# A branch moved ahead of three sums: where TensorE waits for a flag in a fused attention and gated-MLP kernel

## The chip, the cores and the metric

The kernel runs on one core of a Trainium2 chip, as one launch. The metric is the device time of an execution in microseconds; the median of the runs counts. The engines are named as in the profile: PE is TensorE (PEld its weight loads), DVE VectorE, ACT ScalarE, POOL GpSimd, SP SyncE, which here only issues DMAs. Each has a sequencer of its own that reads instructions and queues them for the engine; the profile writes it with a q (PEldq, DVEq).

## The reference, cut to what matters

```python
def reference(A_x, A_wqkv, A_wo, B_x, B_w1, B_w3, B_w2, gate_w):
    x = A_x                                             # 1 x 2048 x 512
    g = _sigmoid((x * gate_w).sum(-1, keepdims=True))
    a = _A_ref(x, A_wqkv, A_wo)   # attention: 32 heads of 16, softmax(q k^T / 4) v, then wo
    b = _B_ref(x, B_w1, B_w3, B_w2) # (silu(x w1) * (x w3)) w2, with F = 1792
    return g * a + (1 - g) * b
```

Both parts are computed from `A_x`. All data is float32.

## The kernel before, in words

The sequence of 2048 rows is cut into 16 tiles of 128 rows (`NT`) and into 4 blocks of 512 columns (`NB`); D = 512 is 4 chunks of 128 (`ND`). Float32 products are made of three matmuls in a faster format: each operand is split into a high and a low half, and `three` (L96, L97, L98) multiplies high by high, high by low and low by high into one PSUM bank.

The first 80 us are a prologue. It loads and transposes x, projects the first 128 columns of Q and K (`project_qk`, L199), and projects V. One V tile is `sums_v(t)`: 4 chunks by `three`, 12 matmuls with 12 weight loads into one of three PSUM banks named `f`. `project_v(t)` lets ACT copy the bank into V (L227). Tiles 0 to 12 go that way; for the last three, 13 to 15, the sums stand in TensorE's order and DVE copies them (L415).

The softmax needs a bound on the scores. `bound` and `guard_rows` work out a bound from norms and write a `flag` (L250): 1 if the bound is at most 64, so that the scores need no exact row maxima. `values_load` (L411) has every engine's sequencer read the flag into a register. `row_maxima` (L293) is a `tc.If(small < 1)` block: where the flag is 0 it projects the rest of Q and K and computes all scores once for their maxima, a body of thousands of TensorE instructions. With these inputs the flag is 1 and every engine branches past the body. On that path each engine passes instructions of one kind, `EVENT_SEMAPHORE`, which wait for the engine's own count and raise the semaphores by what the skipped body would have added (on SP eight of them, for its DMA semaphores).

What follows is the main part, some 1300 us. An order written out by hand as a string of Q, F and P sets TensorE's stream: Q is a pair of score matmuls (L791, with an exponential on ACT at L795), P the products with V (L779), F the matmuls of the remaining projections and of the MLP (L432, L550). The first is Q. The scores read `Kt` and `Qt`, which SP loads with DMAs (L270, L277, and L282 for the guard rows). The kernel is under `tc.manual_schedule()`: each engine gets its instructions in the order of the text.

The lines around the change, before it:

```python
    load_guard(0, 0, 0)                                              # SP, L282
    project_v(12)
    small = nc.values_load(flag, min_val=0, max_val=1)               # L411
    last_v = [sums_v(t) for t in range(NT - 3, NT)]                  # TensorE: 36 matmuls
    row_maxima(small)                                                # the branch, L293
    for to, src in last_v:
        nc.vector.tensor_copy(to, src)                               # DVE, L415
```

Of the kernel before, what the change touches and what calls it, by code (L numbers as in the profile page):

```python
# [24 lines left out]
NT = S // P  # L25
# [8 lines left out]
def gated_mix_kernel(ctx: ExitStack, tc: tile.TileContext, x, wqkv, wo, w1, w3, w2, gate_w, out):  # L34
# [18 lines left out]
    nc = tc.nc  # L53
# [35 lines left out]
    def bank():  # L89
        return psum.tile([P, 512], F32, name="f", bufs=3)  # L90
# [3 lines left out]
    def three(ps, sH, sL, mH, mL, first, last):  # L94

        nc.tensor.matmul(ps, sH, mH, start=first, stop=False)  # L96
        nc.tensor.matmul(ps, sH, mL, start=False, stop=False)  # L97
        nc.tensor.matmul(ps, sL, mH, start=False, stop=last)  # L98
# [120 lines left out]
    def sums_v(t):  # L219
        ps = bank()  # L220
        b, o = divmod(P * t, 512)
        for k in range(ND):
            three(ps, xH[b][:, k, o:o + P], xL[b][:, k, o:o + P], wv[k][0], wv[k][1], k == 0, k == ND - 1)
        return V[:, t, :, 0:DH], ps.rearrange("p (h d) -> p h d", d=DH)
# [184 lines left out]
    load_guard(0, 0, 0)  # L409
    project_v(12)  # L410
    small = nc.values_load(flag, min_val=0, max_val=1)  # L411
    last_v = [sums_v(t) for t in range(NT - 3, NT)]
    row_maxima(small)
    for to, src in last_v:
        nc.vector.tensor_copy(to, src)  # L415
    ph1.close()
    wk = ctx.enter_context(tc.tile_pool(name="wk", bufs=1))

# [503 lines left out]
```

## Time and profile before

| | us |
|---|---|
| median of 3 runs | 1403.82 (1403.74 to 1717.74) |
| the profiled execution | 1402.91 |
| its span, first to last instruction | 1401.1 |
| TensorE busy | 1394.2 |
| ScalarE busy | 1032.8 |
| VectorE busy | 486.6 |
| GpSimd busy | 321.1 |

The profile shows one execution. The highest of the three runs stands apart from the other two, which agree within 0.1 us. Busy time on TensorE counts a matmul from its start to a modelled end, and successive matmuls overlap; whether TensorE waits is read from the starts of its matmuls. Register, branch and semaphore instructions of the sequencers aren't counted as busy; they appear when a line of the source is asked for by itself.

### The profile page before, as it was taken

How to read it: one execution, taken by the hardware profiler on the slowest of the kernel's cores; microseconds unless marked ns; L12 is line 12 of the kernel's file. 1: busy time of each engine (PE TensorE's matmuls, PEld its weight loads, DVE VectorE, ACT ScalarE, POOL GpSimd, SP SyncE). 2: the span in 40 equal slices, each digit the busy share in tenths (PEclk: the TensorE clock that was granted, in tenths of full speed). 3: DMA queues.
4: the chain of work that ended last, by engine and by line, in shares of the span. 5: the costliest groups of instructions: out<-in, count | busy, mean ns of one | idle time of the engine just before them, and what ended most of it. 6: DMA issues, size and time to landing. Idle time of an engine off the chain costs nothing.

```text
span 1401.1 us, 28802 instructions
## 1 busy us (share of the span) xinstructions
PE 1394.2 (100%) x11398; PEld 819.8 (59%) x11398; DVE 486.6 (35%) x1069; ACT 1032.8 (74%) x1153; POOL 321.1 (23%) x357
## 2 busy tenths in 40 slices
PE   9999999999999999999999999999999999999998
PEld 8866566565565565565565565555555555555556
DVE  5511111564545556555464654411111111110013
ACT  4457677777777777777777777788778878877880
POOL 6123433011011101110110117241233232133240
PEclk9999999999999999999999999999999999999999
DMA  7753564343223423223332236444443433355445
GB/s 205 174 121 97 135 135 112 74 112 77 50 54 84 114 55 84 62 67 96 69 77 70 78 80 169 97 99 98 106 96 89 109 102 81 63 127 116 89 136 178
DMA packets 112814, 141.44 MB, mean 101 GB/s; under 512 B 16416, under 2 KB 70944, under 8 KB 109600
## 3 DMA queue, kind: packets, MB, share of 16 engines
q1 hardware_dynamic: 110240, 135.32, 40.8%
q10 hardware_dynamic: 2432, 4.20, 0.9%
q8 instruction: 92, 1.51, 0.5%
q14 instruction: 50, 0.41, 0.1%
HBM read 90.70 MB, written 48.76 MB: 100 GB/s over the span
## 4 chain that ended last, share of the span: by engine, by line
PE 99%; ACT 0%; DVE 0%; issue 0%; DVEq 0%; ACTq 0%
PE acc L779 33%; PE f L432 27%; PE S L791 19%; PE f L550 11%; PE S L199 2%; PE f L96 1%; PE f L98 1%; PE f L97 1%; PE f L636 1%; ACT p L795 0%; PE acc L353 0%; PE f L165 0%; PE S L98 0%; PE S L97 0%; PE S L96 0%; PE S L165 0%
## 5 line engine op out<-in xcount | busy, mean ns | idle before, releaser
L795 ACT ACTIVATE p<-S 128x1024 f32<-128x1024 f32 x1024 | 967.4, 1026 | 298.9 <-PE S L791 289.7
L779 PE MATMUL acc<-p,V 128*17 128x512 f32 x4096 | 474.1, 594 | 0.0
L791 PE MATMUL S<-Qt,Kt 50*128 50x512 f32 x2048 | 402.7, 408 | 1.2 <-DVE V L415 0.7
L791 PEld LDWEIGHTS S<-Qt,Kt 50*128 50x128 f32 x2048 | 183.1, 184 | 186.3 <-ACT p L795 85.7
L779 PEld LDWEIGHTS acc<-p,V 128*17 128x17 f32 x4096 | 102.2, 97 | 272.2 <-issue 272.2
L463 DVE RECIPROCAL sg<-sg 128x64 f32<-128x64 f32 x448 | 209.1, 517 | 49.3 <-issue 47.3
L432 PE MATMUL f<-xL,fh 64*128 64x512 f32 x1088 | 218.0, 392 | 0.0
L432 PE MATMUL f<-xH,fl 64*128 64x512 f32 x1088 | 218.0, 392 | 0.0
L432 PE MATMUL f<-xH,fh 64*128 64x512 f32 x1088 | 217.1, 390 | 0.0
L432 PEld LDWEIGHTS f<-xH,fl 64*128 64x128 f32 x1088 | 104.9, 186 | 24.0 <-POOL fl L329 0.4
L432 PEld LDWEIGHTS f<-xL,fh 64*128 64x128 f32 x1088 | 105.1, 186 | 22.4
L432 PEld LDWEIGHTS f<-xH,fh 64*128 64x128 f32 x1088 | 104.3, 185 | 23.4
L752 DVE MEMSET tick<- 1x1 f32 x189 | 11.2, 59 | 272.8 <-PE f L550 155.0
L328 POOL CAST fh<-fr 128x512 fp32r<-128x512 f32 x34 | 21.6, 637 | 357.2 <-DMA fr<-in_B_w_dram 233.4
L455 DVE COPY gs<-f 128x512 f32<-128x512 f32 x56 | 38.7, 691 | 69.0 <-PE f L432 62.8
L550 PE MATMUL f<-xL,fh 64*128 64x512 f32 x208 | 61.8, 390 | 0.0
L550 PE MATMUL f<-xH,fl 64*128 64x512 f32 x208 | 60.8, 390 | 0.0
L550 PE MATMUL f<-xH,fh 64*128 64x512 f32 x208 | 59.9, 390 | 0.0
L550 PE MATMUL f<-xH,raw 64*128 64x512 f32 x192 | 57.4, 390 | 0.0
L461 DVE TENSOR_SCALAR sg<-sg 128x512 f32<-128x512 f32 x56 | 27.2, 485 | 81.7 <-ACT sg L460 79.6
L619 POOL TENSOR_TENSOR hx<-hx,gw 128x512 f32<-128x512 f32 x8 | 10.3, 1288 | 197.3 <-DMA gw<-r_d 186.7
L760 DVE COPY u<-acc 128x512 f32<-128x512 f32 x32 | 22.1, 692 | 96.1 <-PE acc L779 81.7
(230 smaller groups left out, 1281.4 us busy)
## 6 DMA issues: line engine op xcount, KB each, us to landing
Kt<-kH_d SPq DMA_DIRECT2D x128, 128.0 KB
h_d<-sg SPq DMA_DIRECT2D x56, 256.0 KB
sg<-h_d SPq DMA_DIRECT2D x43, 256.0 KB
fr<-in_B_w_dram SPq DMA_DIRECT2D x42, 256.0 KB
Qt<-qH_d SPq DMA_DIRECT2D x128, 64.0 KB
Kt<-kL_d SPq DMA_DIRECT2D x64, 128.0 KB
Qt<-qL_d SPq DMA_DIRECT2D x64, 64.0 KB
b_d<-y SPq DMA_DIRECT2D x16, 256.0 KB
```

The lines of the kernel that those rows point to most:

```text
L96: nc.tensor.matmul(ps, sH, mH, start=first, stop=False)
L199: nc.tensor.matmul(ps[:, i, :], w[i][h][:, k, :], xs[b][:, k, :], start=n == 0, stop=n == len(order) - 1)
L328: nc.gpsimd.tensor_copy(hi, src)
L432: return nc.tensor.matmul(ps, w[i == 1][r, k, :], (xL if i == 2 else xH)[b][r, k, :], start=n == 0 and not second, stop=n == 3 * ND - 1 an ...
L455: nc.vector.tensor_copy(gs, ps)
L461: small.append(lambda: nc.vector.tensor_scalar(sg, sg, 1.0, None, op0=OP.add))
L463: small.append(lambda q=q: nc.vector.reciprocal(sg[:, q:q + 64], sg[:, q:q + 64]))
L550: ins = nc.tensor.matmul(ps, hs[t][q][i == 1][r, P * o:P * o + P], (w2L if i == 2 else w2H)[q][r, o, :], start=n == 0 and not second, stop ...
L760: nc.vector.tensor_copy(u, acc)
L779: nc.tensor.matmul(acc[r:r + DH + 1, :], V[:, k, 2 * j + h, :], p[:, h, :], start=k == 0, stop=k == NT - 1)
L791: nc.tensor.matmul(ps[:, h, :], Kt[i][r:r + 50, P * k:P * k + P], Qt[i][r:r + 50, t:t + 512], start=True, stop=True)
L795: nc.scalar.activation(p, ps, AF.Exp, scale=SCALE)
```

## The change

The three sums move behind the branch, each directly ahead of its copy. The flag's load stays where it was, and the branch now comes directly behind it. The instructions are the same ones.

```diff
     project_v(12)
     small = nc.values_load(flag, min_val=0, max_val=1)
-    last_v = [sums_v(t) for t in range(NT - 3, NT)]
     row_maxima(small)
-    for to, src in last_v:
-        nc.vector.tensor_copy(to, src)
+    for t in range(NT - 3, NT):
+        nc.vector.tensor_copy(*sums_v(t))
     ph1.close()
```

## The prediction

> **What bounds the kernel now.** The page comes first: its span, the share of TensorE (PE), and the chain of work that ended last.
>
> ```profile
> span 1401.1 us, 28802 instructions
> ...
> PE 1394.2 (100%) x11398; PEld 819.8 (59%) x11398; DVE 486.6 (35%) x1069; ACT 1032.8 (74%) x1153; POOL 321.1 (23%) x357
> ...
> PE 99%; ACT 0%; DVE 0%; issue 0%; DVEq 0%; ACTq 0%
> ```
>
> TensorE works from end to end and the chain is 99% TensorE. So time can only move where TensorE stands idle, and an idle microsecond that appears or goes near 70 us moves everything behind it one for one. The timeline around the branch comes next (start, length, engine, line, idle time before it):
>
> ```profile
> 70.91 0.39 PE L98 MATMUL f<-vh,xL 128*128 128x512 f32 x1
> 71.14 0.39 PE L96 MATMUL f<-vh,xH 128*128 128x512 f32 x1
> ...
> 79.07 0.39 PE L98 MATMUL f<-vh,xL 128*128 128x512 f32 x1
> 79.50 0.69 DVE L415 COPY V<-f 128x512 f32<-128x512 f32 x1 [1.53 <-PE f L98]
> ...
> 80.15 0.58 PEld L791 LDWEIGHTS S<-Qt,Kt 50*128 50x128 f32 x4 [1.12 <-issue]
> 80.18 0.99 PE L791 MATMUL S<-Qt,Kt 50*128 50x512 f32 x4 [0.72 <-DVE V L415]
> ```
>
> 70.91 is the last matmul of V tile 12. The 36 matmuls of tiles 13 to 15 start from 71.14 to 79.07, one every (79.07 - 71.14) / 35 = 0.227 us. The first score could have started at 79.07 + 0.23 = 79.30 and starts at 80.18: **0.88 us idle**. That gap is the whole visible price of the branch today. The page blames the DVE copy, but the weight load at 80.15 starts before that copy is over (79.50 + 0.69 = 80.19). I therefore read the gap as TensorE's own waits behind the branch, and go to the rows of the flag's load (L411) and of the branch (L293), which name the sequencers (a q behind the engine; "PEldq" is TensorE's):
>
> ```profile
> L411 POOLq TENSOR_LOAD <-flag x1: 963/963/963, 63.5 to 63.5; - x1
> L411 PEldq TENSOR_LOAD <-flag x1: 1289/1289/1289, 67.1 to 67.1; - x1
> ...
> L293 SPq EVENT_SEMAPHORE  x8: 17/17/17, 77.9 to 78.4; - x8
> L293 POOLq COMPARE_BRANCH  x1: 45/45/45, 64.5 to 64.5; - x1
> L293 POOLq EVENT_SEMAPHORE  x1: 17/17/17, 64.7 to 64.7; - x1
> L293 DVEq COMPARE_BRANCH  x1: 72/72/72, 71.3 to 71.3; - x1
> L293 ACTq COMPARE_BRANCH  x1: 45/45/45, 71.9 to 71.9; - x1
> L293 ACTq EVENT_SEMAPHORE  x1: 17/17/17, 72.1 to 72.1; - x1
> L293 SPq COMPARE_BRANCH  x1: 50/50/50, 74.4 to 74.4; - x1
> L293 PEldq COMPARE_BRANCH  x1: 3739/3739/3739, 75.2 to 75.2; - x1
> L293 DVEq EVENT_SEMAPHORE  x1: 21/21/21, 76.6 to 76.6; - x1
> L293 PEldq EVENT_SEMAPHORE  x1: 51/51/51, 79.5 to 79.5; - x1
> ```
>
> Three facts. First, TensorE's sequencer runs ahead of its array: it takes up the flag's load at 67.1, when (70.91 - 67.1) / 0.227 = 17 matmuls are still to start, and the branch at 75.2, again 17 before 79.07. Second, its branch costs 3.74 us, 75.2 to 78.9, and today that lies wholly under those 17 matmuls, the last of which ends at 79.07 + 0.39 = 79.46. Third, the long branch is a fetch of instructions. POOL and ACT, with little in the skipped body, go on 0.2 us behind their branch; DVE, SP and PE, whose skipped bodies are long, go on 5.3 us (71.3 to 76.6), 3.5 us (74.4 to 77.9) and 3.7 us behind theirs. A transfer of instructions, 16 KB, falls into PE's branch: the first row below is the queue's answer for 75.9 to 76.5, 13.4% of 16 engines in 0.6 us, so 1.29 us long; the second, for 70.5 to 72.3, shows another one of 4.8% x 16 x 1.8 = 1.38 us.
>
> ```profile
> q8 instruction: 1, 0.02, 13.4%
> ...
> q8 instruction: 1, 0.02, 4.8%
> ```
>
> [...]
>
> **The change part by part.** On DVE, ACT, POOL and SP nothing changes place: they have the load, the branch and the copies in the same order as before. Only TensorE's stream changes: its branch, now behind 36 matmuls and their weight loads, comes directly behind the flag's load, with the 36 behind it. No instruction and no DMA is added or taken away.
>
> 1. *When the branch starts.* The flag's load keeps its place, 67.1 + 1.289 = 68.4. POOL's branch came within 0.05 us of its load's end (63.5 + 0.963 = 64.46, branch at 64.5), so PE's branch starts at 68.4.
>
> 2. *What covers it.* At 68.4 only the rest of tiles 11 and 12 is queued, and its last matmul ends at 70.91 + 0.39 = 71.30: 2.9 us of cover, where there were 4.2 (79.46 - 75.2). The 1.29 us of the load have eaten into the same 17 matmuls that the branch had to itself. So a branch of 3.74 us doesn't fit any more.
>
> 3. *How long the branch is there.* This the trace doesn't show for 68.4. What differs is the traffic (DMA share and GB/s in the last two columns):
>
> ```profile
> 68.00:70.00 2.00, 2.00 (x10) 1.66 (x9) 1.83 (x6) 0.67 (x2) 0.00 (x0) 1.00 1.01 207
> 70.00:72.00 2.00, 2.00 (x10) 1.68 (x9) 0.60 (x3) 0.76 (x2) 0.00 (x0) 1.00 1.05 208
> 72.00:74.00 2.00, 2.00 (x10) 1.65 (x10) 0.00 (x0) 0.00 (x0) 0.00 (x0) 1.00 1.20 168
> 74.00:76.00 2.00, 2.00 (x11) 1.65 (x10) 0.00 (x0) 0.00 (x0) 0.00 (x0) 1.00 0.32 45
> 76.00:78.00 2.00, 2.00 (x11) 1.65 (x10) 1.29 (x2) 0.00 (x0) 0.00 (x0) 1.00 0.06 12
> ```
>
> Until 74 us the 16 DMA engines are full (the loads of Kt and of the guard rows); from 76 they are empty. PE's and SP's branches fetched in the quiet, DVE's (71.3) was caught in the full stretch and took 5.3 instead of SP's 3.5: 1.8 us more. PE's branch moves from the quiet stretch into the full one. Bounds: below, 0.2 us as for POOL and ACT, if nothing had to be fetched; above, a fetch that gets no engine before the data are through. Those end about 74 + 0.32 x 2 = 74.6, and a quiet branch goes on 3.74 - (76.2 - 75.2) = 2.7 us behind the start of its transfer, so 74.6 + 2.7 = 77.3. I take the nearest row, DVE's, and add its 1.8 to PE's own 3.74: **5.5 us**, so the branch ends at 68.4 + 5.5 = 73.9.
>
> 4. *From the branch to the first matmul.* ACT needs 72.1 - 71.9 = 0.2 from branch to semaphore; PE's first weight load comes a step later. I take 0.3 together: tile 13 starts at **74.2** instead of 71.14, 3.1 us late. The 36 matmuls keep their 0.227 us each.
>
> 5. *What is given back.* The first score's waits now meet a sequencer that is again about 17 matmuls ahead, so they are passed while tile 15 is summed: the 0.88 us go. SP's eight semaphores (77.9 to 78.4), for which the scores wait, are there in time: the score's slot is 74.2 + 36 x 0.227 = 82.4, and its waits come up about 3.9 us earlier, at 78.5. The copies stay covered: DVE comes out of its branch at 76.6, and tile 13 is ready at 74.2 + 12 x 0.227 + 0.2 = 77.1; the last copy ends about 0.7 us into the scores, and the first two blocks of the other products use the banks of tiles 13 and 14. Were this cover gone, it would cost one copy, 0.7 us.
>
> Sum: 3.1 - 0.88 = **+2.2 us**. On the profiled execution, 1402.91 us around a span of 1401.1, that gives 1405.1; the median of the runs, 1403.82, lies 0.9 above the profiled one, so I forecast 1403.82 + 2.2 = **1406.0 us**. A difference under about 2% (28 us) can't be told from no change by a measurement of this kernel's kind: the forecast is no change, a little on the slow side.
>
> **The rivals.**
>
> *Quiet fetch.* The instruction queue passes the data queue: the transfer that started in the full stretch (4.8% row) was no longer than the quiet one, 1.38 against 1.29 us. Then the branch takes 3.74, ends at 72.1, tile 13 starts at 72.4, and the sum is 1.3 - 0.9 = +0.4: 1404.2. Against it: what DVE lost was before its transfer, not in it.
>
> *The branch costs nothing there.* If TensorE's target needn't be fetched, as with POOL and ACT (0.2 us), tile 13 is on time and only the 0.88 us go: 1402.9, faster than before. Against it stand PE's 3.74 us in this very place; only where the block were already held would it happen. [...]
>
> *The clock drops: the slow side.* One mechanism: the idle stretch from 71.30 grows until TensorE's granted clock is halved.
>
> ```profile
> 1.55 3.01 PE L353 MATMUL acc<-ident 128*128 128x128 f32 x13 [1.55 <-DVE acc L349]
> ...
> 6.67 1.26 PE L353 MATMUL acc<-ident 128*128 128x128 f32 x10
> ...
> 1396.64 0.39 PE L98 MATMUL S<-wo,p 128*128 128x512 f32 x1
> ...
> 1400.00:1401.00 1.00, 0.00 (x0) 0.00 (x0) 0.00 (x0) 0.00 (x0) 0.00 (x0) 0.76 0.00 0
> ```
>
> After the last matmul (1397.0) the clock falls to half for 0.48 of the microsecond from 1400 (mean 0.76), so at about 1400.5, 3.5 us later. At the start, 13 transposes take 3.01 us (0.23 each), later 10 take 1.26 (0.13): half speed by their spacing for about 3 us, 1.5 us lost. Here it decides from an idle stretch of 3.5 us, a first matmul at 74.8 or later, a branch of 6.1 us or more: 0.6 above my value, and the bound of 77.3 is well past it. Price: with tile 13 at 74.8, +2.8 and 1.5 for the clock, +4.3; at the bound (77.6), +5.6 and 1.5, +7.1: 1408.1 to 1410.9. [...]
>
> *The change does nothing on TensorE*, if what builds the program had put the sums ahead of the branch there again: 1403.8. The program is emitted in the order of its text (the kernel asks for a manual schedule), which leaves little room for it.
>
> **How the numbers follow.** Forecast (branch 4.5 to 6.1 us, +1.2 to +2.8): 0.50. Quiet fetch (+0.2 to +1.2): 0.20. Late fetch, with or without the clock (+2.8 to +7.1): 0.22. Costs nothing (-0.9): 0.04. Nothing changes (0): 0.02. Something outside these, with over 2% on either side: 0.02, for no row here holds 28 us. The range from 1403.6 to 1410.0 leaves out the two small cases and the far end of the late fetch. Faster by over 2% 0.01, within 2% 0.97, slower by over 2% 0.02.
>
> **What would show it.** PE's branch row at 68.4 with 5 to 6 us; a hole on PE from 71.3 to about 74.2, put down to issue or to the branch; the first score directly behind tile 15 at about 82.4, without 0.88 us of idle time; the rows of DVE, ACT, POOL and SP at their old times; clock 1.00 throughout. A branch row of about 3.7 proves the quiet fetch, a clock under 1.00 near 75 the third rival. I am wrong altogether if the scores then wait for something that 8 us of sums had hidden, a load of Kt or SP's semaphores.

## The result and the profile after

| | before | after |
|---|---|---|
| median of 11 executions | 1403.82 us | 1407.29 us (1404.54 to 1408.21) |
| profiled execution | 1402.91 us | 1404.54 us |
| its span | 1401.1 us | 1402.8 us |

The ratio is 1.0021, with a 95% interval of 1.0013 to 1.003: 3 us slower (3.47 us between the two medians), which is clear of no change and far inside 2%. The profiled execution is the fastest of the eleven. It shows the mechanism, but not all of the median; that is what the experiments were for.

First the rows of the branch's line in the changed kernel, in the form read before:

```profile
L293 PEldq COMPARE_BRANCH  x1: 5072/5072/5072, 68.3 to 68.3; - x1
L293 DVEq COMPARE_BRANCH  x1: 72/72/72, 71.2 to 71.2; - x1
...
L293 PEldq EVENT_SEMAPHORE  x1: 51/51/51, 73.4 to 73.4; - x1
L293 SPq COMPARE_BRANCH  x1: 50/50/50, 74.0 to 74.0; - x1
L293 DVEq EVENT_SEMAPHORE  x1: 21/21/21, 76.3 to 76.3; - x1
...
  PE f L96: 2.4, 1
```

TensorE branches at 68.3 instead of 75.2, and the branch takes 5.07 us instead of 3.74. DVE and SP are where they were. The last line is from the list of those who waited for this line: the first matmul behind it, 2.4 us. The timeline of TensorE shows the hole and its end:

```profile
70.80 0.39 PE L98 MATMUL f<-vh,xL 128*128 128x512 f32 x1
73.56 0.47 PE L96 MATMUL f<-vh,xH 128*128 128x512 f32 x1 [2.37 <-PEq L293]
...
81.61 0.39 PE L98 MATMUL f<-vh,xL 128*128 128x512 f32 x1
81.93 0.74 PE L790 MATMUL S<-Qt,Kt 50*128 50x512 f32 x4
...
88.87 3.63 PE L778 MATMUL acc<-p,V 128*17 128x512 f32 x32
```

Tile 12 ends, nothing starts for 73.56 - 71.03 = 2.5 us beyond its slot, and the first score follows tile 15 after 0.32 us instead of 1.11. The last row, the first product with V, is the mark by which the kernels are compared below. Before, it was this one:

```profile
87.25 3.63 PE L779 MATMUL acc<-p,V 128*17 128x512 f32 x32
```

From the last matmul of tile 12 to this mark it is 87.25 - 70.91 = 16.34 us before and 88.87 - 70.80 = 18.07 after: **+1.73 us at the branch**. Behind the mark both need 1309.4 us to their last matmul.

### The profile page after: what moved, and what is told of

Read it like the earlier page. It is cut to its first block, busy times and chain, and to the rows that moved or that the text cites. A ratio compares the mean times of both kernels' runs of the same rounds, so it can differ in the third digit from the quotient of the medians.

```text
span 1402.8 us, 28802 instructions
## 1 busy us (share of the span) xinstructions
PE 1394.2 (99%) x11398; PEld 819.8 (58%) x11398; DVE 485.7 (35%) x1069; ACT 1032.7 (74%) x1153; POOL 320.9 (23%) x357
## 3 DMA queue, kind: packets, MB, share of 16 engines
q8 instruction: 91, 1.49, 0.5%
## 4 chain that ended last, share of the span: by engine, by line
PE 94%; ACT 0%; DVE 0%; issue 0%; DVEq 0%; ACTq 0%
PE acc L778 33%; PE f L431 27%; PE S L790 19%; PE f L549 11%; PE f L635 1%; PE f L96 1%; PE f L98 1%; PE f L97 1%; ACT p L794 0%; PE S L98 0%; PE S L96 0%; PE S L97 0%; PE f L642 0%; PE acc L98 0%; PE acc L96 0%; PE acc L97 0%
## 5 line engine op out<-in xcount | busy, mean ns | idle before, releaser
L568 DVE SCALAR_TENSOR_TENSOR y<-f,omg,y 128x512 f32<-128x512 f32 x32 | 23.9, 748 | 90.1 <-PE f L549 90.1
```

Of the source, the lines that this page charges most:

```text
L568: nc.vector.scalar_tensor_tensor(y, ps, omg[:, t:t + 1], y, op0=OP.mult, op1=OP.add)
```

## Experiments

The theory is the forecast's: a fetch of instructions that was hidden under queued matmuls, lengthened by data traffic, is no longer hidden. *Cover* means the time from the branch's start to the end of the last matmul queued ahead of it, the *hole* the idle time of TensorE behind that matmul, and the *mark* the first product with V. The rival for what the profile doesn't explain, some 2 us in most executions, is the clock.

**The changed kernel again** (`a_again`), no edit, to get the profile of another execution.

> The changed kernel once more. Its first profiled execution took 1404.54 us with a branch of 5.07 us on TensorE and a hole of 2.4 us, but most of its other executions took 1406.9 to 1408.2, some 2.5 us more. Theory (traffic): the branch's fetch waits for the data loads, by a varying length; in an execution of about 1407 the branch's row is 7 to 8 us, tile 13 starts near 76, the granted clock stays 1.00. Rival (clock): the branch stays at 5 to 6 us, but the hole lets the clock drop, so that matmuls behind it come every 0.43 us for some 3 us and the clock's mean between 74 and 80 is under 1.00. Second rival: the 2.5 us come from somewhere behind 90 us; then the first score starts at 81.9 in this profile too. Median 1405 to 1408 by all three.

Measured: median 1407.03 us beside 1403.60 (ratio 1.0024, 1.0014 to 1.0033); the profiled execution took 1406.86. Its branch row, timeline and stretches (the third figure from the end is the granted clock):

```profile
L293 PEldq COMPARE_BRANCH  x1: 5072/5072/5072, 69.0 to 69.0; - x1
```

```profile
71.43 0.39 PE L98 MATMUL f<-vh,xL 128*128 128x512 f32 x1
74.21 0.77 PE L96 MATMUL f<-vh,xH 128*128 128x512 f32 x1 [2.40 <-PEq L293]
74.78 0.63 PE L97 MATMUL f<-vl,xH 128*128 128x512 f32 x1
75.20 0.63 PE L98 MATMUL f<-vh,xL 128*128 128x512 f32 x1
...
77.34 0.53 PE L97 MATMUL f<-vl,xH 128*128 128x512 f32 x1
77.70 0.39 PE L98 MATMUL f<-vh,xL 128*128 128x512 f32 x1
77.93 0.40 PE L96 MATMUL f<-vh,xH 128*128 128x512 f32 x1
...
91.10 3.63 PE L778 MATMUL acc<-p,V 128*17 128x512 f32 x32
```

```profile
72.00:74.00 2.00, 0.00 (x0) 0.00 (x0) 0.00 (x0) 0.45 (x1) 0.00 (x0) 1.00 0.95 139
74.00:76.00 2.00, 1.79 (x4) 1.49 (x5) 0.00 (x0) 0.00 (x0) 0.00 (x0) 0.55 0.65 94
76.00:78.00 2.00, 2.00 (x7) 1.57 (x6) 0.00 (x0) 0.00 (x0) 0.00 (x0) 0.59 0.01 4
78.00:80.00 2.00, 2.00 (x11) 1.63 (x10) 0.69 (x1) 0.00 (x0) 0.00 (x0) 1.00 0.13 37
```

The branch and the hole are the same to 0.03 us. What differs is the clock: half speed for (1 - 0.55) x 4 + (1 - 0.59) x 4 = 3.4 us, with matmuls every 0.43 us instead of 0.23. From tile 12 to the mark it is 91.10 - 71.43 = 19.67 us, 1.60 more than in the other profile: 3.4 us hold 8 matmuls at 0.43 us, and each of them lost 0.20. Most of the rest of the difference between the two profiles, 0.63 us, lies ahead of tile 12 (71.43 against 70.80), and that varies from profile to profile (see the end). Of the 22 executions of this kernel 17 took 1406.5 us or more and 5 took 1404.3 to 1405.5. The drop was traced in one of the 17. Their mean granted clock fits it, 0.999 in all 17 and 1.000 in three of the five, so the median very probably belongs to the kind with the drop. In the traced execution the clock rival holds; the longer branch and the place behind 90 us fall.

**The flag's load one tile earlier** (`early_load`):

```diff
-    project_v(12)
     small = nc.values_load(flag, min_val=0, max_val=1)
+    project_v(12)
     row_maxima(small)
```

> The changed kernel with the flag's load one tile earlier, ahead of the sums of tile 12, and the branch where the change put it. Theory (cover and clock): the load's 1.26 us no longer eat into the queued matmuls, so TensorE's branch starts near 70.91 - 17 x 0.227 = 67.1 instead of 68.3 and has 4.2 us of cover instead of 2.9; it takes 5.0 to 6.0 us (the data queue is as full), the hole is 1.1 to 2.0 us instead of 2.4, too short for the clock to drop in most executions: median 1404.0 to 1405.0 beside 1403.6 for the kernel before. If cover doesn't matter or the clock drops at any hole: 1406 to 1407, as with the change itself.

Measured: median 1403.55 us beside 1403.78 (0.9996, 0.9986 to 1.0005).

```profile
L293 PEldq COMPARE_BRANCH  x1: 4246/4246/4246, 68.1 to 68.1; - x1
```

```profile
72.50 0.47 PE L96 MATMUL f<-vh,xH 128*128 128x512 f32 x1 [0.17 <-PEq L293]
```

The hole is gone but for 0.17 us, no execution took over 1403.93, and tile 12 to the mark takes 15.87 us, 0.47 less than before the change. With the load's 1.26 us out of the way the 17 queued matmuls hide a branch of 4.2 us. That is not cover alone: of the 2.2 us of hole that went, 1.4 are cover (72.32 - 68.1 = 4.2 us instead of 2.9), and 0.8 are a branch shorter than the 5.07 of the changed kernel and than expected. The DMA engines were nearly as full from 68 to 72 us (shares 0.97 and 1.01 instead of 1.07 and 1.09); why the branch was shorter stays open.

**Less data moving at the branch** (`quiet`): the changed kernel with

```diff
-    load_k(0, 0)            # ahead of project_v(11)
-    load_guard(0, 0, 0)     # ahead of project_v(12)
     row_maxima(small)
+    load_k(0, 0)
+    load_guard(0, 0, 0)
```

> The changed kernel with the loads of Kt and of the guard rows moved behind the branch, so that fewer data move when TensorE's branch fetches. The loads come late, so the whole gets slower (the first score some 8 us later); what is read is the branch's row. Theory (traffic): TensorE's branch takes 3.7 to 4.2 us instead of 5.1, DVE goes on 3.5 us behind its branch instead of 5.1, and the executions agree within 0.5 us. If traffic has nothing to do with it: TensorE's branch stays at 5 us or more.

Measured: median 1404.24 us beside 1403.60 (1.0004, 0.9995 to 1.0014), all executions between 1403.3 and 1405.0.

```profile
L293 PEldq COMPARE_BRANCH  x1: 4172/4172/4172, 69.6 to 69.6; - x1
...
L293 DVEq COMPARE_BRANCH  x1: 72/72/72, 72.5 to 72.5; - x1
...
L293 DVEq EVENT_SEMAPHORE  x1: 21/21/21, 75.4 to 75.4; - x1
```

```profile
70.00:72.00 2.00, 2.00 (x10) 1.65 (x10) 1.61 (x7) 0.60 (x2) 0.00 (x0) 1.00 0.61 127
72.00:74.00 2.00, 0.51 (x4) 0.12 (x2) 0.04 (x1) 0.60 (x1) 0.00 (x0) 1.00 0.02 8
```

0.9 us off TensorE's branch with the same cover, a hole of 1.49 us, and no sign of the clock drop. TensorE's row alone doesn't settle the traffic: the share was still 0.87 from the branch at 69.6 until its transfer started at 71.4, and `early_load` has 4.25 us under fuller engines. DVE's branch is the clearer reading. It starts at 72.5, when the engines have just run empty, and DVE goes on 2.9 us later, where the changed kernel needed 76.3 - 71.2 = 5.1. The executions spread over 1.7 us instead of the expected 0.5. The expected 8 us of lateness didn't come: SP, which no longer waits for the guard rows, left its own branch sooner, and Kt was there when the sums were done.

**More data moving at the old place** (`busy_before`): the kernel before, with 6 more loads of 128 KB.

```diff
     project_v(12)
+    for h in range(2):
+        for o in range(3):
+            r = 64 * h + DH * o
+            nc.scalar.dma_start(Kt[1][r:r + DH, :].bitcast(F32), QD[1][o // 2][DH * h:DH * h + DH, :])
```

> The kernel before, with the branch behind the three sums, and 6 more transfers of 128 KB (K rows into the second Kt tile, which the next step overwrites) from ScalarE's queue behind tile 12, so that the DMA engines are still moving data when TensorE branches at 75.2. What is read is the branch's row; the first score may come later because SP's semaphores wait for these transfers. Theory (traffic): the branch takes 4.5 to 6 us instead of 3.7 and its transfer starts 1.5 us or more behind the branch instead of 1.0. If the place of the branch and not the traffic made 5.1 us of it: 3.7 us again.

```profile
L293 PEldq COMPARE_BRANCH  x1: 5878/5878/5878, 75.1 to 75.1; - x1
```

```profile
74.00:76.00 2.00, 2.00 (x11) 1.65 (x10) 0.69 (x1) 0.00 (x0) 0.00 (x0) 1.00 1.01 131
76.00:78.00 2.00, 2.00 (x10) 1.68 (x9) 0.69 (x1) 0.00 (x0) 0.00 (x0) 1.00 1.02 135
...
82.00:84.00 2.00, 0.00 (x0) 0.00 (x0) 0.00 (x0) 0.00 (x0) 0.00 (x0) 0.79 0.30 45
```

With the DMA engines full (1.01, 1.02 instead of 0.32, 0.06) the branch in its old place takes 5.88 us instead of 3.74. Its transfer starts at 77.6, 2.5 us behind the branch instead of 1.0, and lasts 1.6 us instead of 1.3. So here traffic lengthened the fetch, mostly by its wait for a start (1.5 of 2.1 us). DVE's branch shows the reverse in the same profile: at its old time, 71.2, but with a share of 0.37 from 70 to 72 instead of 1.05, DVE goes on after 3.1 us instead of 5.3. The whole (1412.3 us, one execution) is about something else: SP's semaphores came 8 us late, and TensorE then stood still for 7.2 us and had its clock halved again.

**A near target** (`short_body`, and once more as `short_before`): the changed kernel with the body of the skipped block left out but for one transpose and the reload.

```diff
         with tc.If(small < 1):
-            for c in range(1, ND):
-                ...
+            idle(1)
             load_step(0)
```

> The changed kernel with nearly the whole skipped body left out: one transpose and the reload of the first step remain in it, so that every engine still branches (with these inputs the body isn't run). Theory (fetch): with a near target nothing has to be fetched; TensorE's branch takes 0.1 to 0.3 us, there is no hole and no drop of the clock, and the 0.88 us ahead of the first score are gone: 1402.5 to 1403.0. If the branch itself costs the time, wherever its target lies: 5 us in its row and 1407 as with the change.

> The changed kernel with the short skipped body once more. Its branch took 0.24 us and it still measured 1405.8 us, 2.0 us over the kernel before, with the loss spread over the whole span in steps of about 0.1 us, one every 76 us. If that belongs to this program: the same steps and 1405 to 1406.6. If it belonged to those runs: 1402.5 to 1404.5 without steps. At the branch itself both expect 0.4 us between tile 12 and tile 13, the time in which TensorE's last matmul ends, its own count is waited for and the first weights are loaded.

```profile
L293 PEldq COMPARE_BRANCH  x1: 236/236/236, 70.2 to 70.2; - x1
```

Measured: branch 0.24 and 0.35 us, no hole, 15.80 and 15.82 us from tile 12 to the mark. The fetch theory holds: with the long body gone, and with it the distance of the target, the price is gone too. Two things came otherwise. At the branch the kernel gains 0.53 us, not 0.88. And the whole was slower, 1405.82 us (ratio 1.0015, 1.0006 to 1.0025) and 1405.35: against the kernel before it loses 0.1 us about every 76 us, 1.8 us behind the mark, in both profiles. The same steps stand in `busy_before`, which has the long body. Their cause stays open; they lie all along the main part, not at the branch.

**One sum, and half a sum, behind the branch** (`one_behind`, `half_behind`, `half_again`). `one_behind` sums tiles 13 and 14 ahead of `row_maxima` and tile 15 behind it; the half kernels also sum the first two chunks of tile 15 ahead of it. The edit shown is that of the half kernels.

```diff
-    last_v = [sums_v(t) for t in range(NT - 3, NT)]
+    last_v = [sums_v(t) for t in range(NT - 3, NT - 1)]
+    sums_v(NT - 1, range(2))
     row_maxima(small)
     for to, src in last_v:
         nc.vector.tensor_copy(to, src)
+    nc.vector.tensor_copy(*sums_v(NT - 1, range(2, ND), half_ps[0]))
```

> Two sums ahead of the branch, one (tile 15) behind it. The branch starts when tile 14's last instructions are queued, 75.2 - 12 x 0.227 = 72.5, while data still move (until 74.6), with 4.2 us of queued matmuls as cover. Theory (traffic): the branch takes 4 to 5 us and ends at 76.5 to 77.5; tile 14 ends at 76.7; tile 15 starts 0.4 to 1.3 us late, the 0.88 us ahead of the first score go: 1403.3 to 1404.3. If the fetch cost the same everywhere (3.7 us): 1403.3. If any sum behind the branch costs what three cost: 1405.5 to 1407.

> Two sums and the first half of tile 15 (6 matmuls) ahead of the branch, the second half behind it. The branch starts at 75.2 - 6 x 0.227 = 73.9 and ends at 77.6 to 78.2; the last matmul queued ahead of it ends at 78.1. What is then left is TensorE's wait for its own last matmul: theory (traffic) expects 0.3 to 0.5 us of idle time ahead of the second half and none ahead of the first score, 0.4 us less than before: 1403.3 to 1403.6. If the 0.88 us of before don't go when sums follow the branch: 1404.2 or more.

> The kernel with two and a half sums ahead of the branch once more, with more rounds: 6 matmuls behind the branch took 0.3 us of idle time ahead of them and none ahead of the first score. If that is all, it is 0.4 to 0.6 us faster than the kernel before (1403.1 beside 1403.6 at first), a ratio of 0.9996, near what the rounds can resolve; if it was a matter of the runs, the medians agree within 0.1 us.

`one_behind`: 1404.34 us beside 1403.60 (1.0004, 0.9995 to 1.0013); its branch came at 73.7 with the DMA engines still full (0.95 and 0.97 from 72 to 76) and took 5.06 us, tile 15 started 79.02 - 77.58 - 0.23 = 1.2 us late, tile 12 to the mark took 16.76 us, +0.42. This is the clean comparison for the cover: beside the changed kernel the branch has the same length, the cover is 4.2 us instead of 2.9, and the hole is 1.06 us instead of 2.37. The half kernel: 1403.09 beside 1403.60, then 1403.05 beside 1403.78 (0.9996, 0.9987 to 1.0005); 15.82 us to the mark in both profiles, 0.52 less than before. Its branch came at 73.9 and took 3.78 us, and at 74.3 and 3.92 in the second profile, so it fitted under the cover. The first of these began while the engines were still full, 0.91 until its transfer started 1.0 us later; so the share at the branch's start doesn't by itself set the wait. The timeline at the branch:

```profile
77.74 0.39 PE L98 MATMUL f<-vh,xL 128*128 128x512 f32 x1
78.28 0.47 PE L96 MATMUL f<-vh,xH 128*128 128x512 f32 x1
...
79.50 0.39 PE L98 MATMUL f<-vh,xL 128*128 128x512 f32 x1
79.82 0.73 PE L796 MATMUL S<-Qt,Kt 50*128 50x512 f32 x4
```

0.54 us from one matmul to the next across the branch instead of 0.23, then a score without a wait. It and `early_load` are the fastest here; both beat the kernel before by half a microsecond at the branch, which their measured totals can't tell from none.

**More traffic with the change** (`busy_after`): 8 copies of K rows from ScalarE's queue ahead of `project_v(12)`.

> The changed kernel with 8 more transfers of 128 KB (copies of K rows into the second Kt tile, which the next step overwrites) from ScalarE's queue ahead of tile 12, so that the DMA engines stay full some 4 us longer. Theory (traffic and clock): TensorE's branch takes 6 to 9 us instead of 5.1, the hole is 3.4 us or more, and now the clock drops in every execution: median 1409 to 1413, none of the executions under 1407. If the fetch doesn't wait for data: branch 5.1 us, median 1407 with some executions at 1404.5.

Inconclusive for traffic: the branch took 4.35 us, not the expected 6 to 9, but the run didn't bring it more data. The transfers waited for others' semaphores on ScalarE's queue, so less data moved at the branch (share 0.62 from 66 to 68); ScalarE's copy of a V tile came behind them, and that made a hole of its own:

```profile
85.37 0.79 PE L96 MATMUL f<-vh,xH 128*128 128x512 f32 x1 [7.62 <-ACT V L227]
```

The median of 1414.97 us (1.008, 1.0064 to 1.0095) is that hole and 10.2 us of half clock around it.

## Why the prediction was right, and where it was off

Forecast 1406.0, range 1403.6 to 1410.0; measured 1407.29. The direction, the mechanism at the branch and the range held; one step failed. That the range holds the median is in part luck: at +3.5 us it lies above the forecast's own case (+1.2 to +2.8), in the part of the range that was kept for a late fetch, while the fetch measured was shorter than forecast. The prediction also said that less than 2% can't be told from no change; the interval here does tell 0.2%.

- *When the branch starts, what covers it*: 68.4 and 2.9 us forecast; 68.3 and 71.19 - 68.3 = 2.9 measured. The prediction's way of counting holds in every profile whose hole the branch makes: the hole is the branch less its cover and 0.2 us more. Branch, cover and hole are 5.07, 2.87 and 2.37 us in the changed kernel, 4.17, 2.85 and 1.49 in `quiet`, 5.06, 4.23 and 1.06 in `one_behind`, 4.25, 4.24 and 0.17 in `early_load`.
- *How long the branch is*: 5.5 forecast, 5.07 measured in both profiles. Taking DVE's branch as the row for traffic was right in kind: TensorE's takes 5.88 us with more data at the old place, and DVE itself goes on after 2.9 and 3.1 us where there is less. The quiet-fetch rival (3.74 us) falls. The size isn't explained by the traffic share alone (4.25 in `early_load`). Even with the short body TensorE's row is longer, 236 and 352 ns, than DVE's 72 and SP's 50.
- *From the branch to the first matmul*: 0.3 forecast; 68.3 + 5.07 = 73.4 to 73.56, 0.2.
- *What is given back*: 0.88 forecast; 2.53 of hole less 1.73 net is 0.80. The first score follows tile 15 after 0.32 us, not after 0.23. The rival that costs nothing was mis-sized too: even behind a near branch tile 13 starts 0.3 us late (73.03 - 72.49 - 0.23 in `short_body`), so the most to be had is 0.5, not 0.88.
- *The sum*: +2.2 forecast, +1.73 in the execution without a clock drop. Most of the difference is the branch, 0.4 us shorter than taken.
- *The clock* is the step that failed. The prediction let it decide from 3.5 us of idle time, read from the one drop that the trace of before shows, at its end, and so put it beyond the forecast. In `a_again` a hole of 2.4 us was enough, for 1.6 us, and by their times it very probably was in 16 more of the 22 executions. With it the sum is +3.3, against +3.5 and +3.4 in the medians. The drop needed no longer branch: it came at the forecast's branch length, and the prediction had tied it to one of 6.1 us or more. Its sign for this rival, a clock under 1.00 near 75 us, did appear.

## What to carry to other kernels

In this kernel a branch on TensorE over a long block cost a fetch of 3.7 to 5.9 us, and it was hidden only where that many microseconds of matmuls were queued ahead of it: put it where the queue is full and the DMA engines are quiet (at one place it took 3.74 us with them quiet and 5.88 with them full), and keep the load of its flag well away from it (directly ahead, its 1.26 us left 2.9 us of cover instead of 4.2). A hole of 2.4 us cost another 1.6 us through the clock, and one profiled execution missed that: look at the spread of the runs, and take a second profile when it has two heaps.

## What the runs showed of the hardware that I had not expected

In these profiles the clock's changes lie on a grid. Its half-speed stretches lasted 3.41 us (`a_again`), 6.83 (`busy_before`) and 10.24 (`busy_after`), one, two and three times the same length of 3.41, and in `a_again` the drop at 74.21 us came 20 such lengths after the trace's first clock record, at 5.94. TensorE was not idle for the whole of the length ahead of two of the drops: in `a_again` that length ran from 70.79 to 74.21 and held matmuls until 71.82, 1.0 of its 3.4 us, so 2.4 us of it were idle. In `busy_after` it ran from 76.35 to 79.77 and held matmuls until 77.75, so 2.0 us of it were idle. In the first profile of the changed kernel 20 lengths from the first record, at 4.61, end at 72.88, with 1.7 us idle in the last of them, and the clock stayed. So a drop was measured behind 2.0 and 2.4 us of idle time in one length, and none behind 1.7. In `quiet` and `one_behind`, with holes of 1.5 and 1.1 us, the clock stayed as well.

Where the grid falls changes from execution to execution, and that also moves the start of the kernel. The first clock record, a rise to full, lies between 4.5 and 7.3 us in these profiles, and until then TensorE works at half speed by the spacing of its transposes (in the kernel before 0.22 us up to its record at 4.47, 0.11 later). In the ten profiles with the long body tile 12's last matmul starts at 70.8 us where that record is early and up to 72.1 where it is late. The two with the short body come some 0.6 us later than that (71.8 and 72.5); why stays open.
